# Sparse attention and a sentence-level mixture of experts on one core: k and q loaded by two head pairs at a time, in another order of the work

## The chip, the cores and the metric

The kernel runs on one core of one Trainium2 chip. The metric is the device time of one execution in microseconds. A profile of one execution stands beside it; its span runs from the first to the last instruction of the program, and all times inside it count from the start of that span.

## The reference

There are 4 batches, 8 heads, 768 positions and a head dimension of 64. Attention looks at near positions and at block summaries:

```python
k_sum = k.reshape(B, H, nb, block, D).max(axis=3)      # block = 32, so nb = 24
v_sum = v.reshape(B, H, nb, block, D).mean(axis=3)
mask_l = np.abs(pos[:, None] - pos[None, :]) < window   # window = 16
scores_s = scale * np.einsum('bhsd,bhnd->bhsn', q, k_sum) + np.log(block)
...
a = softmax of [masked scores_l, scores_s];  out = a @ [v, v_sum]
```

The heads side by side are x (768 x 512 for each batch). A gate takes the mean of x over positions, multiplies it by a 512 x 8 matrix and picks one expert for the whole batch; the output is the gate's probability times relu(x W1) W2 of that expert, with W1 512 x 1024 and W2 1024 x 512. So the weights of a batch's expert can only be fetched when its attention is complete.

## The kernel before, in words

All work is cut into 622 (634 after the change) small operations. The function `Plan` (lines 85 to 168) holds them; a list of numbers, `ORDER` (line 22), gives the order in which they are emitted. `solve` walks that list with a planned duration for each operation; it decides which buffer of a pool an operation takes, whether ACT or DVE does it where both may, and how many idle matmuls (line 880, they keep TensorE busy) go ahead of an operation that the plan finds waiting. It doesn't reorder. Each engine then runs its own operations in the order of the list, and waits at the head of its queue for what is missing.

The operations of a batch, with the lines that profiles show:

- Loads on POOL's queue: k and q rows (`load_rows`, L241), v (`load_v`, L252), and after the gate the expert's weights in five pieces (`G_load`, W1 in three pieces, L754, W2 in two, L757). The weights' pieces hold feature groups 0 to 1, 2 to 3 and 4 to 7 of W1. Loads are issued in the fixed order of `FIRST` and `LOADS` (lines 1096 and 1097): for each batch k and q, then v, then the weights of the batch before. Every load casts float32 to bfloat16.
- `T_pair` (L419): for one pair of heads, 16 transposes of k and 16 of q on PE. It waits for the loads of its own pair only. `K_own` and `Q_all` (L429 on ACT, L431 on DVE) copy the two results out of PSUM; `K_rest` (L461 to L481, DVE) takes the block maxima and fills in borders. Batch 0 uses `T` (L403), `K_max` and `S_mm` (L560 to L582) in their place.
- `S_win` (L602): the scores of one pair and one half of the positions, into the only score buffer of PSUM. `S_exp` (L621, ACT) is the exponential, `S_mask` (L368, DVE) the window.
- `V_sum` (L519, PE), `V_out`, `V_edge` (L501, L503) and `V_copy` (L542): the block means of v, put beside v.
- `O_mm` (L637, PE), `O_norm` (L651, L656, DVE), `X_mm` (L671, PE), `X_out` (L680, ACT, with the sum over positions): the attention's output, normalized and transposed.
- The gate: `G_add` (L698, DVE, batch 0 alone), `G_mm` (L707, PE), `G_pick` (L720 to L731 on DVE, then one small exponential, L736, on ACT). Their place on ACT and DVE is that of `G_pick` in the list. The plan counts no time on ACT for it. `factors` (L359 to L361) and `blocks` (L381 to L388) are constants that DVE builds once.
- The expert: `H_mm` (L786, 4 matmuls for one feature group and one half of the positions, 16 such groups), `H_out` (relu, L805 on ACT, L803 on DVE), `Y_mm` (L814, half of the features for 128 rows, called half-Y below), `Y_out` (L833, L828), `Y_store` (L871, SP). The last 128 rows of batch 3 go out in two halves (`Z_mm` L843, `Z_out` L862 and L863). `G_bc` (L772, SP) spreads the gate's value over 128 partitions.

The attention of batch b+1 is mixed with the expert of batch b. Six PSUM buffers of the pool "one" serve everything but scores; a PE operation that takes one waits until its last user has copied it out. k and q have two buffers each, by batch.

The part that the change touches reads, before:

```python
if kind == "kq":
    loads_kq(b, "k", ALLP, 0.8, KQ)
    loads_kq(b, "q", ALLP, 0.8, KQ)
```

Of the kernel before, what the change touches and what calls it, by code (L numbers as in the profile page):

```python
# [19 lines left out]


ORDER = [
    19, 14, 0, 2, 3, 1, 20, 22, 5, 29, 15, 4, 6, 23, 8, 21, 31, 30, 7, 24, 33, 17, 9, 10,
    38, 25, 32, 26, 34, 40, 12, 47, 18, 35, 16, 98, 56, 11, 36, 99, 58, 37, 57, 60, 39, 27,
    49, 78, 42, 59, 13, 41, 100, 50, 48, 74, 79, 66, 28, 67, 43, 61, 44, 75, 51, 45, 70,
    101, 68, 63, 62, 64, 80, 82, 65, 46, 52, 71, 69, 72, 53, 86, 102, 103, 83, 54, 84, 90,
    81, 104, 73, 87, 55, 91, 76, 94, 95, 108, 77, 88, 85, 96, 92, 89, 109, 97, 105, 126,
    110, 93, 171, 172, 111, 112, 106, 117, 107, 173, 113, 120, 127, 128, 118, 114, 119, 175,
    177, 115, 176, 135, 144, 129, 121, 136, 145, 122, 116, 178, 187, 137, 185, 138, 179,
    147, 146, 123, 151, 193, 186, 149, 152, 148, 195, 124, 194, 180, 181, 125, 183, 153,  # L30
    139, 188, 140, 189, 203, 248, 196, 156, 141, 157, 182, 250, 207, 190, 150, 184, 205,
    154, 191, 142, 252, 130, 204, 143, 208, 215, 158, 249, 206, 131, 197, 155, 216, 132,
    133, 166, 167, 199, 211, 192, 209, 251, 253, 134, 168, 200, 213, 212, 161, 210, 201,
    198, 174, 254, 169, 170, 162, 159, 238, 202, 218, 160, 163, 164, 165, 265, 239, 319,
    268, 214, 320, 321, 256, 266, 267, 323, 274, 255, 219, 325, 269, 259, 324, 327, 329,
    275, 217, 257, 220, 228, 258, 270, 233, 326, 277, 283, 260, 276, 229, 240, 261, 234,
    286, 271, 328, 292, 284, 235, 272, 285, 331, 273, 333, 339, 230, 262, 293, 337, 334,
    297, 296, 263, 347, 294, 396, 335, 336, 278, 330, 264, 338, 279, 348, 295, 223, 340,
    355, 351, 304, 280, 298, 224, 352, 341, 281, 305, 282, 299, 287, 356, 225, 345, 300,
    398, 342, 301, 288, 359, 363, 309, 289, 346, 364, 306, 290, 310, 302, 243, 332, 307,  # L40
    357, 360, 311, 353, 291, 244, 303, 308, 354, 314, 400, 245, 358, 315, 246, 397, 399,
    343, 413, 344, 404, 416, 316, 414, 402, 422, 415, 361, 317, 405, 322, 401, 362, 365,
    381, 349, 407, 221, 318, 236, 425, 417, 350, 247, 418, 376, 312, 382, 419, 226, 377,
    403, 313, 386, 423, 241, 424, 227, 467, 468, 406, 469, 471, 420, 426, 378, 427, 231,
    431, 440, 441, 421, 442, 434, 473, 475, 383, 445, 470, 408, 477, 366, 409, 444, 242,
    391, 222, 387, 371, 232, 388, 410, 392, 237, 432, 472, 367, 452, 411, 433, 443, 428,
    453, 393, 481, 372, 429, 482, 412, 435, 474, 493, 485, 368, 430, 436, 479, 476, 454,
    373, 495, 483, 446, 494, 478, 496, 505, 497, 484, 498, 374, 457, 506, 458, 486, 447,
    384, 437, 509, 448, 369, 438, 491, 513, 487, 511, 510, 501, 449, 492, 450, 439, 488,
    462, 459, 512, 489, 460, 451, 502, 480, 455, 463, 503, 490, 394, 461, 499, 464, 389,  # L50
    456, 379, 465, 500, 385, 504, 524, 466, 544, 519, 514, 545, 390, 507, 546, 395, 370,
    508, 548, 539, 529, 540, 380, 515, 534, 525, 535, 520, 547, 526, 375, 549, 530, 550,
    551, 527, 562, 516, 560, 536, 552, 558, 531, 553, 541, 554, 566, 559, 563, 572, 582,
    568, 583, 528, 567, 570, 584, 569, 521, 571, 556, 561, 522, 588, 564, 586, 585, 578,
    587, 555, 565, 573, 523, 557, 574, 542, 532, 517, 579, 576, 606, 589, 601, 580, 575,
    518, 537, 596, 590, 591, 597, 533, 581, 598, 577, 599, 538, 607, 592, 543, 600, 611,
    608, 609, 602, 593, 612, 613, 594, 619, 620, 610, 616, 595, 603, 604, 614, 617, 605,
    615, 621, 618,
]


# [20 lines left out]
class Plan:  # L82
# [16 lines left out]
    def add(self, engs, fn, kind, prio, deps=(), takes=(), count=0):  # L99
        if isinstance(engs, tuple):  # L100
            engs = [engs]
        op = Op(engs, fn, prio, deps, takes)
        op.kind, op.count = kind, count
        op.idx = len(self.ops)
        self.ops.append(op)
        for s in op.takes:
            s.users.append(op)
        return op
# [64 lines left out]
def kernel(  # L173
# [64 lines left out]
    def load_rows(b, which, src, h0, h1):  # L238
        if (which, b) not in nat:
            nat[which, b] = ld.tile([PR, H, RR * D], BF16, name=f"{which}_nat")  # L240
        nc.gpsimd.dma_start(  # L241
            nat[which, b][:, h0:h1, :],
            src[b, h0:h1].rearrange("h (p r) d -> p h (r d)", r=RR),
        )
# [77 lines left out]
    def edges(i):  # L322

        def f(op):
            e = nc.gpsimd
            e.memset(kaugs[i][:, :, 0:1, 0:R_OWN], 0.0)
            e.memset(kaugs[i][:, :, NJ - 1 : NJ, R_POST:R_SUM], 0.0)
            e.memset(kaugs[i][:, :, :, NR:128], 0.0)
        return f
# [570 lines left out]
    def transfer(fn, issue, dur, deps=()):  # L900

        deps = list(deps)
        if len(lanes) >= 8:
            deps.append(lanes[-8])
        if last[0] is not None:
            deps.append(last[0])
        i = add(("pool", issue), fn, "load", 0, deps)
        last[0] = i
        q_ = add(("q", dur), None, "ring", 0, [i])
        lanes.append(q_)  # L910
        return i, q_

    def loads_kq(b, which, prs, issue, per):
        deps = [R["T" + which, b - 2, p] for p in range(NP) if b >= 2]
        src = {"k": k, "q": q}[which]
        _, t = transfer(
            lambda op: load_rows(b, which, src, 2 * prs[0], 2 * prs[-1] + 2),
            issue, per * len(prs), deps,
        )
        for p in prs:  # L920
            R["L" + which, b, p] = t

    def loads_v(b, prs, issue, per):
        deps = [R["O", b - 2, p, u] for p in prs for u in range(2) if b >= 2]
        deps += [R["Vs", b - 2, p] for p in prs if b >= 2]
        _, t = transfer(
            lambda op: load_v(b, 2 * prs[0], 2 * prs[-1] + 2),
            issue, per * len(prs), deps,
        )
        for p in prs:  # L930
            R["Lv", b, p] = t

    KQ, VV = 1.1, 2.25
    ALLP = list(range(NP))
# [93 lines left out]
    def gate(b):  # L1028
        gs = Slot("one")
        a = add(("dve", 0.1), G_add(b), "gate", -1000,  # L1030
                [R["x", b, p, u] for p in ALLP for u in range(2)])
        m = add(("pe", 0.25), G_mm(b), "gate", -1000, [a], [gs])
        p = add(("dve", 0.6), G_pick(b), "gate", -1000, [m])
        gs.users.append(p)
        rec = add(("dve", 0.15), G_rec(b), "gate", -900, [p])
        R["grec", b] = rec
        w = Slot("w")
        R["w", b] = w
        deps = [p]
        for i, (c0, c1) in enumerate(zip(W1CUTS, W1CUTS[1:])):  # L1040
            iss, t = transfer(G_load(b, 0, c0, c1), 2.2 if i == 0 else 0.8,
                              1.05 + 0.4 * (c1 - c0), deps)
            if i == 0:
                iss.takes.append(w)
                w.users.append(iss)
            for c in range(c0, c1):
                R["w1", b, c] = t
        for c in range(2):
            _, t = transfer(G_load(b, 1, 4 * c, 4 * c + 4), 0.8, 2.6)
            R["w2", b, c] = t  # L1050
# [66 lines left out]
    def load_now(what):  # L1117
        kind, b = what[:-1], int(what[-1])
        if kind == "e":
            for i in (0, 1):  # L1120
                R["edge", i] = last[0] = add(("pool", 1.2), edges(i), "load", 0, [last[0]])
            return
        if kind == "kq":
            loads_kq(b, "k", ALLP, 0.8, KQ)
            loads_kq(b, "q", ALLP, 0.8, KQ)
        elif kind in ("k", "q"):
            loads_kq(b, kind, ALLP, 0.8, KQ)
        elif kind == "v":
            loads_v(b, [0, 1], 2.2, VV)
            loads_v(b, [2, 3], 2.2, VV)  # L1130
        else:
            gate(b)
# [5 lines left out]
    for what in LOADS:  # L1138
        load_now(what)
        if what[:-1] in after:  # L1140
            after[what[:-1]](int(what[-1]))
# [32 lines left out]
```

## Time and profile before

| what | value |
|---|---|
| median of 3 runs | 163.21 us (162.63 to 163.76) |
| the profiled execution's own time | 163.21 us |
| its span | 161.5 us |
| mean granted TensorE clock | 0.983 |
| k and q loads of batches 1 to 3 | 6 of 768 KB, median 14.5 us (k) and 17.6 us (q) from issue to landing |
| v of batch 0, second half, landed | 22.5 us |
| gate matmuls of batches 0 to 3 (L707) | 34.0, 61.2, 98.0, 127.2 us |
| first expert matmul, end of the last matmul | 41.2 us, 157.2 us |
| idle matmuls (L880) | 48, 14.5 us busy |

In the profile PE is TensorE's matmuls, PEld its weight loads, DVE VectorE, ACT ScalarE, POOL GpSimd and SP SyncE; a "q" behind a name is that engine's instruction queue. "128x512<-128x512 x18 | 12.4, 687" reads: output and input sizes, 18 instructions, 12.4 us busy in all, 687 ns each. An arrow in brackets names what ended a wait. The slices of the page are 40 equal parts of the span, and a digit is a share in tenths.

### The profile page before, as it was taken

What the parts mean: (1) busy time and instruction counts of PE and PEld (TensorE: products, weight loads), DVE (VectorE), ACT (ScalarE), POOL (GpSimd) and SP (SyncE); (2) the same over time, 40 slices, a digit from 0 to 9 for tenths busy, and PEclk for the clock granted to TensorE, in tenths of its full rate; (3) what the DMA queues carried; (4) which work ended last, traced back from release to release, by engine and by line L of the source; (5) the groups of instructions that cost most, each with busy time, mean ns of one, the idle gap of its engine ahead of it and who ended that gap; (6) DMA issues with size and microseconds to landing.
All of it is one profiled execution on the core that took longest, in us unless ns stands there. A gap on an engine that the chain in (4) does not pass through costs nothing.

```text
span 161.5 us, 4894 instructions
## 1 busy us (share of the span) xinstructions
PE 148.8 (92%) x2088; PEld 87.9 (54%) x2088; DVE 101.4 (63%) x288; ACT 90.3 (56%) x170; POOL 41.2 (26%) x58
## 2 busy tenths in 40 slices
PE   6798979989999997999999995999999999999990
PEld 2354657665556665555565753645667445565450
DVE  4387799679996844999786985686686231431010
ACT  3233447678778667796766764546668305352430
POOL 6997300009930001991000001700000080000000
PEclk9999999999999999999999999599999999999997
DMA  2999999998999999999999991999750059996135
GB/s 17 197 173 164 149 199 201 154 126 92 150 204 207 208 169 138 163 199 198 206 205 158 144 341 53 123 151 207 224 212 4 0 69 140 224 253 227 60 136 195
DMA packets 58581, 26.01 MB, mean 161 GB/s; under 512 B 38976, under 2 KB 55616, under 8 KB 58560
## 3 DMA queue, kind: packets, MB, share of 16 engines
q0 software_dynamic: 53856, 19.40, 132.2%
q1 hardware_dynamic: 4704, 6.31, 11.2%
q8 instruction: 16, 0.26, 0.7%
q14 instruction: 5, 0.04, 0.1%
HBM read 38.81 MB, written 6.29 MB: 279 GB/s over the span
## 4 chain that ended last, share of the span: by engine, by line
PE 70%; DMA 14%; POOL 4%; ACT 3%; issue 3%; DVE 2%; POOLq 0%; DVEq 0%; ACTq 0%
PE hps L786 24%; PE o_ps L814 21%; DMA vblk<-in_v_dram 9%; DMA w_sb<-in_moe_w_dram 5%; PE tps L419 5%; PE ops L637 4%; PE sc L602 4%; PE xps L671 4%; PE vsps L519 3%; PE idle_ps L880 3%; POOL vblk L252 1%; ACT aT L621 1%; PE o_ps L843 1%; POOL k_nat L241 1%; POOL q_nat L241 1%
## 5 line engine op out<-in xcount | busy, mean ns | idle before, releaser
L786 PE MATMUL hps<-xT,w_sb 128*128 128x384 bf16 x256 | 46.0, 327 | 0.2 <-DMA w_sb<-in_moe_w_dram 0.2
L814 PE MATMUL o_ps<-w_sb,hT 128*128 128x512 bf16 x184 | 43.9, 385 | 0.0
L621 ACT ACTIVATE aT<-sc 128x768 bf16<-128x768 f32 x32 | 25.9, 808 | 14.4 <-PE sc L582 8.8
L786 PEld LDWEIGHTS <-w_sb 128*128 128x128 bf16 x256 | 23.4, 98 | 15.8 <-DMA w_sb<-in_moe_w_dram 0.6
L754 POOL DMA_DIRECT2D w_sb<-in_moe_w_dram x12 | 9.0, 759 | 90.1 <-DVE kmt L461 37.3
L805 ACT ACTIVATE hT<-hps 128x384 bf16<-128x384 f32 x44 | 21.0, 491 | 15.3 <-PE hps L786 15.2
L814 PEld LDWEIGHTS <-hT 128*128 128x128 bf16 x184 | 17.2, 99 | 18.8 <-issue 1.1
L833 ACT ACTIVATE o_sb<-o_ps,gcol 128x512 f32<-128x512 f32 x18 | 12.4, 687 | 13.7 <-PE o_ps L814 13.6
L803 DVE TENSOR_SCALAR hT<-hps 128x384 bf16<-128x384 f32 x20 | 10.8, 554 | 14.3 <-PE hps L786 14.3
L656 DVE TENSOR_TENSOR xs<-ops,rv 128x384 bf16<-128x384 f32 x32 | 17.8, 558 | 1.1
L680 ACT ACTIVATE xT<-xps 128x768 bf16<-128x768 bf16 (+1 forms) x20 | 13.5, 681 | 5.0 <-PE xps L671 5.0
L252 POOL DMA_DIRECT2D vblk<-in_v_dram x10 | 15.8, 1596 | 0.8 <-issue 0.8
L880 PE MATMUL idle_ps<-zb 128*128 128x512 bf16 x48 | 14.5, 428 | 1.6 <-DVE zb L272 1.3
L368 DVE TENSOR_TENSOR aT<-aT,seen 96x1536 bf16<-96x1536 bf16 x12 | 11.3, 950 | 1.8 <-ACT aT L621 1.7
L429 ACT COPY qT<-tps 128x768 bf16<-128x768 bf16 x13 | 10.3, 793 | 0.9 <-PE tps L403 0.5
L602 PE MATMUL sc<-qT,kaug 64*128 64x64 bf16 x288 | 8.5, 193 | 2.3 <-ACT aT L621 2.3
L828 DVE TENSOR_SCALAR o_sb<-o_ps,gcol 128x512 f32<-128x512 f32 x5 | 3.7, 747 | 10.9 <-PE o_ps L814 10.9
L651 DVE RECIPROCAL rv<-ops 128x6 f32<-128x6 f32 x32 | 6.1, 190 | 6.6 <-PE ops L637 6.2
L637 PEld LDWEIGHTS <-aT 120*64 120x64 bf16 x384 | 7.6, 111 | 4.5 <-issue 3.3
L602 PEld LDWEIGHTS <-kaug 64*128 64x128 bf16 x288 | 5.8, 96 | 7.7 <-issue 6.4
L542 DVE COPY vblk<-vs_sb 24x1536 bf16<-24x1536 bf16 x16 | 9.7, 611 | 0.4
L637 PE MATMUL ops<-vblk,aT 120*64 120x65 bf16 x384 | 9.7, 197 | 0.3 <-DVE vblk L503 0.3
(93 smaller groups left out, 163.4 us busy)
## 6 DMA issues: line engine op xcount, KB each, us to landing
w_sb<-in_moe_w_dram POOLq DMA_DIRECT2D x12, 512.0 KB, 9.9
out_dram<-o_sb SPq DMA_DIRECT2D x23, 256.0 KB, 3.4
vblk<-in_v_dram POOLq DMA_DIRECT2D x6, 576.0 KB, 21.8
k_nat<-in_k_dram POOLq DMA_DIRECT2D x3, 768.0 KB, 14.5
q_nat<-in_q_dram POOLq DMA_DIRECT2D x3, 768.0 KB, 17.6
w_sb<-in_moe_w_dram POOLq DMA_DIRECT2D x8, 256.0 KB, 5.2
vblk<-in_v_dram POOLq DMA_DIRECT2D x2, 564.0 KB, 16.8
k_nat<-in_k_dram POOLq DMA_DIRECT2D x2, 384.0 KB, 5.6
```

The lines of the kernel that those rows point to most:

```text
L252: nc.gpsimd.dma_start(vb[p0:p1, n0:n1, 0:D], bass.AP(v.tensor, v.offset + ((b * H * NJ + n0) * QB - HALO + p0) * D, [[D, p1 - p0], [QB * D ...
L368: nc.vector.tensor_tensor(out=rows, in0=rows, in1=seen.unsqueeze(1).to_broadcast([R_SUM, 2 * NJ, QB]), op=ALU.mult,)
L602: nc.tensor.matmul(sc[:, hh, w * QB : (w + 1) * QB], lhsT=ka[rs, pr, j, :], rhs=qT[rs, j * QB : (j + 1) * QB], start=True, stop=True, tile ...
L621: nc.scalar.activation(aT, scs.pop((b, pr, u)), ACT.Exp, scale=SCALE)
L637: nc.tensor.matmul(ops[w * QB : (w + 1) * QB, t, hh, :], lhsT=weights(b, pr, hh, j), rhs=vb[0:NR, 2 * pr + hh, j, 0 : D + 1], start=True, ...
L656: nc.vector.tensor_tensor(out=xss[s][:, t0 : t0 + NW // 2], in0=ops[:, :, :, 0:D], in1=rv.unsqueeze(3).to_broadcast([128, NW // 2, 2, D]), ...
L680: nc.scalar.activation(xT[b][:, pr, us[0] * HB : (us[-1] + 1) * HB], xpss.pop((b, pr, us[0])), ACT.Copy, accum_out=red[b][:, pr, us[0] : u ...
L786: nc.tensor.matmul(hps[:, 0:HB], lhsT=w1_sb[:, dt, ft * 128 : (ft + 1) * 128], rhs=xT[b][:, dt, u * HB : (u + 1) * HB], start=(dt == 0), s ...
L805: nc.scalar.activation(dst, hps[:, 0:HB], ACT.Relu)
L814: nc.tensor.matmul(o_ps, lhsT=hTs[b][:, ft, st * 128 : (st + 1) * 128], rhs=wts[b][1][:, ft, :], start=(ft == 0), stop=(ft == NFT - 1),)
L833: nc.scalar.activation(o_sb, o_ps, ACT.Copy, scale=gcols[b][:, 0:1])
L880: nc.tensor.matmul(idle_ps[0], lhsT=zb[:, 0:128], rhs=zb, start=True, stop=True)
```

## The change

For batches 1 to 3 the loads of k and q go by two head pairs: k of pairs 0 and 1, q of pairs 0 and 1, k of pairs 2 and 3, q of pairs 2 and 3. There are four loads of 384 KB for each of these batches in place of two of 768 KB. Since the operations' numbers shift, and since the list was found again, `ORDER` is another list throughout, with 634 entries in place of 622; the operations on PE, ACT, DVE and SP are the same in number and kind but for one idle matmul fewer (47). Some go to ACT in place of DVE or the other way, as `solve` decides.

```diff
 ORDER = [
-    19, 14, 0, 2, 3, 1, 20, 22, 5, 29, 15, 4, 6, 23, 8, 21, 31, 30, 7, 24, 33, 17, 9, 10,
...
-    615, 621, 618,
+    19, 14, 0, 2, 1, 29, 3, 4, 5, 31, 6, 8, 30, 15, 21, 16, 32, 33, 7, 20, 22, 34, 10, 38,
...
+    606, 621, 616, 628, 607, 610, 611, 622, 629, 617, 612, 631, 630, 632, 633,
 ]
...
         if kind == "kq":
-            loads_kq(b, "k", ALLP, 0.8, KQ)
-            loads_kq(b, "q", ALLP, 0.8, KQ)
+            for prs in ([0, 1], [2, 3]):
+                loads_kq(b, "k", prs, 0.75, KQ)
+                loads_kq(b, "q", prs, 0.75, KQ)
```

The changed order on PE around the gates, written by operation (b.p is batch and pair; "half-Y" is one `Y_mm`):

```
batch 2 first:  ... O 1.2, H, O 1.3, T 2.0, X 1.1, half-Y, H, X 1.2, H, X 1.3, half-Y, half-Y, S 2.0,
                T 2.2, T 2.1, gate 1, S 2.0, T 2.3, 5 half-Y, S 2.1, V_sum 2, ...
batch 3 first:  ... O 2.3, T 3.0, half-Y, H, H, H, half-Y, S 3.0, T 3.1, X 2.1, X 2.3, half-Y, T 3.2, S 3.0,
                half-Y, half-Y, gate 2, S 3.1, half-Y, T 3.3, S 3.1, 4 half-Y, V_sum 3, S 3.2, ...
```

In the order before, the gates' surroundings are:

```
gate 1:  ... T 2.1, half-Y, gate 1, T 2.0, T 2.2, half-Y, S 2.1, ...
gate 2:  ... S 3.1, half-Y, half-Y, gate 2, S 3.2, T 3.3, V_sum 3, ...
```

On DVE the block maxima of pair 3 of batch 0 move behind `V_edge` of pairs 2 and 3, and `factors` from the start to between the sum and the pick of gate 0. The instructions on ACT, in the changed order, after the exponential of gate 2 are a k copy of pair 3 and an exponential of pair 1; the two ahead of it are a k copy of pair 2 and an exponential of pair 1.

## The prediction

> **What bounds the kernel now.** I read the page's busy table and slices first, then the chain that ended last, then the timeline around the chain's pauses, then the granted clock by window. The busy table and the slices:
>
> ```profile
> PE 148.8 (92%) x2088; PEld 87.9 (54%) x2088; DVE 101.4 (63%) x288; ACT 90.3 (56%) x170; POOL 41.2 (26%) x58
> ...
> PEclk9999999999999999999999999599999999999997
> ```
>
> TensorE is busy 92% of the span and no other engine is above 63%, so time is lost where PE stops or runs slowly. Its clock has one hole, slice 25 (about 101 to 105 us). The chain agrees: after 22.5 us, when the second half of v of batch 0 has landed, it is nearly all PE. From the first expert matmul (L786, 41.24 us) to the last (157.24) PE pauses at few places, nearly all at a gate. The worst is the gate of batch 2; the timeline there (start, duration, engine, line, wait in brackets):
>
> ```profile
> 95.85 0.35 PE L602 MATMUL sc<-qT,kaug 64*128 64x64 bf16 x12
> ...
> 97.96 0.34 PE L707 MATMUL lgps<-wg_sb,red 128*1 128x8 f32 x8
> ...
> 99.04 0.30 ACT L736 ACTIVATE ex<-lg,negm 1x8 f32<-1x8 f32 x1 [3.04 <-DVE negm L731]
> 99.24 0.18 ACT L736 ACTIVATION_READ_ACCUMULATOR ex<-lg,negm 1x1 f32 x1
> 99.34 0.78 ACT L621 ACTIVATE aT<-sc 128x768 bf16<-128x768 f32 x1
> ...
> 100.17 0.35 PE L602 MATMUL sc<-qT,kaug 64*128 64x64 bf16 x12 [1.86 <-ACT aT L621]
> ```
>
> The scores of 95.85 were complete at 96.2, but their exponential stands on ACT behind the gate's own small exponential, which waits for the gate matmul and five DVE steps. There is one score buffer, so PE's next scores wait till 100.17. What follows, by window (PEclk is the column after POOL):
>
> ```profile
> 98.30:100.17 1.87, 0.01 (x1) 0.03 (x1) 0.61 (x6) 1.13 (x4) 0.00 (x0) 1.00 0.04 15
> 100.17:101.70 1.53, 1.53 (x64) 1.41 (x67) 0.97 (x2) 1.21 (x2) 1.40 (x2) 0.87 0.00 0
> 101.70:104.40 2.70, 2.70 (x56) 1.59 (x45) 1.79 (x4) 1.61 (x3) 2.35 (x4) 0.50 1.14 146
> ```
>
> PE is full, at half clock. Price, from the chain: the v sum (48 matmuls) took 1.39 against 0.79 for batch 2, the scores 0.44 against 0.28, the 16 L814 matmuls 4.35 against 2 x 1.73: 0.60 + 0.16 + 0.89 = 1.65 us. The gate of batch 1 does the same to a k copy:
>
> ```profile
> 62.27 0.30 ACT L736 ACTIVATE ex<-lg,negm 1x8 f32<-1x8 f32 x1 [1.08 <-DVE negm L731]
> ...
> 63.40 0.53 PE L419 MATMUL tps<-identb,k_nat 96*64 96x96 bf16 x16 [1.05 <-ACT kaug L429]
> ```
>
> Two more PE pauses, 0.29 at 43.75 and 0.18 at 139.54, complete it: 1.05 + 1.86 + 1.65 + 0.29 + 0.18 = 5.03 us lost after 41.24.
>
> **What the Trainium skill says.** "TensorE: Matmul & The Clock Gate", Part 1, says ACT and DVE are strict FIFO; 99.04 above agrees. The same part gives an activity window of 3413 ns and a half-rate clock after an idle one, warning of gaps above some 3.4 us. Here a gap of 1.86 us was followed by the drop, so the measurement decides; the 1.05 us gap was followed by none. "DMA: Bandwidth & Descriptors", Queues, rings and completion order, says each DMA engine consumes descriptors in ring order; the trace agrees: k of batch 2, issued at 40.22, took 15.1 us to land (55.3), q, issued at 41.01, 18.3 us (59.3), in order, 4.0 us apart. Its Anatomy of one DMA (SWDGE) gives about 2.0 us fixed per DMA, mostly completion latency.
>
> **The change part by part.** (1) *Six more load issues.* k and q of batches 1 to 3 become 12 half loads. On POOL one issue takes 0.68 to 0.83 us (L241 rows), whatever its size, so each batch has 2 more, about 1.5 us, ahead of v. That is hidden: v of batch 2 is issued at 41.78 and lands at 64.2, and POOL waits 18 us or more before each gate's loads (19.1, 18.1, 27.0, 25.8 in the timeline). Without this cover v would be 1.5 us late. Fixed cost per extra DMA is between 0 (latency of queued transfers overlaps) and 2.0 us (that page's figure, an estimate); I take 0, since queued w loads of 512 KB land 2.55 us apart (46.05, 48.61, 51.16).
>
> (2) *What the halves free.* Transposes of pairs 0 and 1 need only the first two half loads. In batch 1 nothing was waiting for them (q lands at 29.5, transposes start at 30.5), in batch 3 neither (85.9 against 88.6). In batch 2 it matters: the new order puts a transpose ahead of the gate's work.
>
> (3) *The order at the gates.* In the changed order ACT has, at gate 2, the exponential of the last scores before the gate, and behind the gate's exponential a k copy that PE needs after two more half-Y groups (ready at 13.1 on the count below, wanted at 14.6) and an exponential that it needs after four and a v sum. Counted from the first transpose of batch 3: PE work up to the gate matmul is 10.15 us; the exponential of the scores ahead of it ends at about 9.3, the next scores' at 11.55, the gate's at 11.95, and PE's next scores come at 12.5. No wait. At gate 1 what stands behind it is a k copy (done about 2 us after the gate matmul), whose buffer PE takes after a transpose and four half-Y groups (over 4 us): no wait. So 1.05 + 1.86 + 1.65 go, and I take the 0.29 and 0.18 as gone too (V_edge and third w1 load have 0.4 and 0.8 us to spare): 5.03.
>
> (4) *Tile switches.* After 41.24 PE changes its tile position 66 times instead of 69; a switch costs 0.11 (first L786 group 0.76, others 0.65): 0.3 gained.
>
> (5) *The tail.* Before, the last output half is queued on SP behind two row stores (157.33, 157.77, then 158.30). Now those come before: issue at about 157.8 in the same frame, 0.5 gained.
>
> (6) *Gate 0 comes later.* The landing of v (22.51) doesn't move, nor does the v sum (done at 24.0). Then on DVE: vs copy 0.41, vblk copy 0.55, edge 0.45, and now also kmx of pair 3 (0.36 + 0.50 + 0.25), so scores of pair 3 start at 26.8 instead of 25.88. At the end DVE has the k copy of batch 1 (0.96), the last norm (0.75), K_rest (1.62), the gate's sum (0.15) and now the factors (0.94 in the timeline, 10.30 to 11.24) before it picks: about 35.1 instead of 34.38, +0.75. Every w load moves by this: first chunk 40.78 to 41.55, second 42.96 to 43.7. First L786: 41.24 to 41.65, +0.4. Its third group wants the second chunk at 43.4: +0.3. The first half loads of batch 2 follow: last w chunk 51.16 + 0.75, plus half of k and of q (2.05 each): 56.0. PE wants them after 14 H (0.65), 5 scores (0.28), 4 O (0.5), one X (0.34) and 7 switches: 13.6 us, at 41.65 + 0.3 + 13.6 = 55.55. Wait 0.5. Loss 1.2; bounds 0.3 (gate not late) to 3.2 (2 us fixed cost on q's half).
>
> (7) *Allowance.* Between 41 and 57 us DVE has 16.4 us of work against 20.5 of PE, with only some 0.4 us to spare at the first O and at two buffers. I charge 0.8, bounds 0 and 2.5.
>
> Sum: -5.03 - 0.3 - 0.5 + 1.2 + 0.8 = -3.8. Span 161.5 - 3.8 = 157.7; the profiled execution took 163.21, 1.7 around the span, and equals the median shown. Prediction 159.4 us.
>
> **Rivals.** *A, the waits move* (0.23): the order meets DVE lateness where I counted 0.4 us of slack; one PE pause of 1.9 us, and the half clock after it (1.65) as at 100 us. For: DVE is above 0.9 busy from 40 to 48 us before. Against: its work there isn't larger than before (16.4 against 16.5). 159.4 + 3.55 = 163.0. *B, slower* (0.14): the half loads share the DMA engines and land together, when q landed before, 59.3 + 0.75 = 60.05. The first transpose of batch 2 stands at PE's head from 55.55: wait 4.5 instead of 0.5, and half clock 1.65 after it: 159.4 + 4.0 + 1.65 = 165.05. It decides from a landing of about 59.8 on. Against: k and q landed in order and apart. *C, better* (0.08): neither (6) nor (7) costs anything: 157.4. *D, the split does nothing* and all is order: same time as mine, since of the split I only charge the 0.5; without it that wait would be B's.
>
> **How the numbers follow.** Likeliest (0.55) 159.4, its own range 158.0 to 161.2; C below, A at 161.6 to 164.5, B above. Leaving out B's upper part and the lowest of C gives 157.9 to 164.6. This kernel's measurement can tell 1% (1.6 us) from no change. Faster: likeliest + C = 0.63; within 1%: A, 0.22; slower 0.15.
>
> **What would show it.** Right: no PE wait on ACT at gates 1 and 2, no slice near 100 us with a low PEclk, gate 0 matmul or its pick 0.5 to 1 us later, first half of q of batch 2 landed near 56. Wrong: a PE pause above 1.5 us anywhere after 42 us with a clock drop behind it, or L419 waiting on q_nat for over 2 us.

## The result, and the profile after

The changed kernel takes 156.96 us (median of 4 runs, 156.71 to 157.40), against 162.92 us of the kernel before in the same runs (162.48 to 163.76): ratio 0.963, 95% interval 0.958 to 0.968. Ratios here and below leave out runs that are more than 1.5% above the fastest of their kernel, so they can differ from the quotient of the medians shown. The direction was as predicted, but the time is 2.4 us below the forecast and 0.9 below the range. The profiled execution took 156.81 us, its span is 154.8: 6.7 less than the span before. The forecast of the span was 157.7, so the miss is 2.9 us there; the forecast put 1.7 us around the span, and the profiled execution has 2.0.

The page after, busy times and granted clock:

```profile
PE 146.1 (94%) x2087; PEld 86.7 (56%) x2087; DVE 100.8 (65%) x291; ACT 89.5 (58%) x167; POOL 44.6 (29%) x64
...
PEclk9999999999999999999999999999999999999999
```

The hole of slice 25 is gone. The busy times by stretch say where 6.7 us went. The stretches are: start to first expert matmul (L786), from there to the end of the last matmul, and the rest. The first numbers are the length, then busy PE, PEld, DVE, ACT and POOL, then the clock. Before:

```profile
0.00:41.24 41.24, 36.18 (x644) 22.36 (x645) 30.79 (x105) 21.20 (x41) 19.87 (x36) 1.00 2.05 147
41.24:157.24 116.00, 112.59 (x1450) 65.53 (x1444) 70.66 (x185) 68.66 (x129) 21.34 (x23) 0.99 1.26 165
157.24:161.50 4.26, 0.00 (x1) 0.00 (x0) 0.00 (x0) 0.47 (x1) 0.00 (x0) 0.75 0.52 185
```

After:

```profile
0.00:40.82 40.82, 35.96 (x644) 22.09 (x644) 29.76 (x105) 22.13 (x41) 21.14 (x38) 1.00 2.01 150
40.82:151.44 110.62, 110.12 (x1450) 64.58 (x1444) 71.03 (x187) 66.91 (x125) 23.50 (x27) 1.00 1.35 175
151.44:154.80 3.36, 0.04 (x1) 0.00 (x0) 0.00 (x0) 0.47 (x1) 0.00 (x0) 1.00 0.43 151
```

The middle stretch is 5.38 us shorter, the start 0.42, the tail 0.90 (0.04 us of the last matmul lies behind the cut at 151.44, and spans are rounded to 0.1, so these sums are good to about 0.1 us). In the middle PE's idle time (length less busy) falls from 116.00 - 112.59 = 3.41 us to 0.50, by 2.91. Its busy time falls by 2.47, of which 1.65 is the half clock as the prediction priced it from the profile of before (no half clock is left after the change); 0.82 is left. Against the prediction's terms:

| part | predicted, us | measured, us |
|---|---|---|
| start to first expert matmul (step 6) | +0.4 | -0.42 |
| PE's pauses after it: -3.38 (step 3), +0.8 (step 6), +0.8 (step 7) | -1.78 | -2.91 |
| half clock (step 3) | -1.65 | -1.65 |
| rest of PE's busy time (step 4) | -0.3 | -0.82 |
| tail (step 5) | -0.5 | -0.90 |
| sum | -3.8 | -6.70 |

The timeline after, at gate 2, answers to the one at 95.85 to 100.17 us before:

```profile
95.94 0.34 PE L707 MATMUL lgps<-wg_sb,red 128*1 128x8 f32 x8
96.22 0.35 PE L602 MATMUL sc<-qT,kaug 64*128 64x64 bf16 x12
...
96.61 0.81 ACT L621 ACTIVATE aT<-sc 128x768 bf16<-128x768 f32 x1 [0.89 <-PE sc L602]
...
97.32 0.28 ACT L736 ACTIVATE ex<-lg,negm 1x8 f32<-1x8 f32 x1
...
98.04 0.80 ACT L429 COPY kaug<-tps 128x768 bf16<-128x768 bf16 x1 [0.35 <-PE tps L419]
...
98.27 0.35 PE L602 MATMUL sc<-qT,kaug 64*128 64x64 bf16 x12
```

ACT has the exponential of the scores ahead of the gate's small one, which finds its input ready (no bracket), and PE's next scores at 98.27 wait for nothing. Of PE's waits, by what ended them (total, times, longest), these two were there before and are not after:

```profile
PE sc L602 <- ACT aT L621: 2.3, 2, 1.9
...
PE tps L419 <- ACT kaug L429: 1.1, 1, 1.1
```

The longest one left after 41 us is new, at the first outputs of batch 1 (47.12 us), behind the window's mask on DVE:

```profile
PE ops L637 <- DVE aT L368: 0.4, 1, 0.4
```

### The profile page after: what moved, and what is told of

Read it like the earlier page. It is cut to its first block, busy times and chain, and to the rows that moved or that the text cites. A ratio compares the mean times of both kernels' runs of the same rounds, so it can differ in the third digit from the quotient of the medians.

```text
span 154.8 us, 4903 instructions
## 1 busy us (share of the span) xinstructions
PE 146.1 (94%) x2087; PEld 86.7 (56%) x2087; DVE 100.8 (65%) x291; ACT 89.5 (58%) x167; POOL 44.6 (29%) x64
## 3 DMA queue, kind: packets, MB, share of 16 engines
q1 hardware_dynamic: 4704, 6.31, 12.2%
## 4 chain that ended last, share of the span: by engine, by line
PE 76%; DMA 9%; DVE 6%; POOL 4%; ACT 1%; issue 1%; POOLq 0%
PE o_ps L814 26%; PE hps L786 25%; DMA vblk<-in_v_dram 9%; PE tps L419 5%; PE ops L637 4%; PE sc L602 4%; PE idle_ps L880 3%; PE xps L671 3%; PE vsps L519 3%; DVE vblk L542 2%; POOL vblk L252 2%; DVE aT L368 1%; PE o_ps L843 1%; POOL k_nat L241 1%; POOL q_nat L241 1%
## 5 line engine op out<-in xcount | busy, mean ns | idle before, releaser
L786 PE MATMUL hps<-xT,w_sb 128*128 128x384 bf16 x256 | 46.5, 327 | 0.0
L814 PE MATMUL o_ps<-w_sb,hT 128*128 128x512 bf16 x184 | 43.2, 379 | 0.0
L786 PEld LDWEIGHTS <-w_sb 128*128 128x128 bf16 x256 | 23.6, 98 | 15.6 <-DMA w_sb<-in_moe_w_dram 0.2
L805 ACT ACTIVATE hT<-hps 128x384 bf16<-128x384 f32 x43 | 20.4, 491 | 17.4 <-PE hps L786 17.2
L833 ACT ACTIVATE o_sb<-o_ps,gcol 128x512 f32<-128x512 f32 x16 | 10.9, 686 | 10.0 <-PE o_ps L814 8.0
L803 DVE TENSOR_SCALAR hT<-hps 128x384 bf16<-128x384 f32 x21 | 11.4, 553 | 7.4 <-PE hps L786 7.0
L828 DVE TENSOR_SCALAR o_sb<-o_ps,gcol 128x512 f32<-128x512 f32 x7 | 5.2, 750 | 13.1 <-PE o_ps L814 12.0
L429 ACT COPY qT<-tps 128x768 bf16<-128x768 bf16 x11 | 8.5, 796 | 1.5 <-PE tps L403 1.5
L651 DVE RECIPROCAL rv<-ops 128x6 f32<-128x6 f32 x32 | 6.1, 189 | 4.8 <-PE ops L637 4.7
L429 ACT COPY kaug<-tps 128x768 bf16<-128x768 bf16 x10 | 7.9, 793 | 1.0 <-PE tps L419 1.0
```

The lines of the kernel that those rows point to most:

```text
L429: nc.scalar.copy(out_, in_)
L786: nc.tensor.matmul(hps[:, 0:HB], lhsT=w1_sb[:, dt, ft * 128 : (ft + 1) * 128], rhs=xT[b][:, dt, u * HB : (u + 1) * HB], start=(dt == 0), s ...
L805: nc.scalar.activation(dst, hps[:, 0:HB], ACT.Relu)
L814: nc.tensor.matmul(o_ps, lhsT=hTs[b][:, ft, st * 128 : (st + 1) * 128], rhs=wts[b][1][:, ft, :], start=(ft == 0), stop=(ft == NFT - 1),)
```

## Experiments

The theory after the result: the gain is the order around the gates on ACT (with the half clock behind it) and the order of SP's last stores, and the prediction's two losses (steps 6 and 7) are covered. Its rivals: the split of the loads brings the gain by itself; something else in the new order does; or step 6 is a real loss that something unseen makes up for. Eight kernels were run, in two groups (E1 to E4, E5 to E8); the kernel before, run beside them, had medians of 164.21 us (39 runs) and 164.02 (23 runs), higher than above, so ratios and spans are compared, not medians of different groups.

**E1, the changed order with whole loads.** The list of operations stays; k and q of batches 1 to 3 are loaded whole in the place of their first halves.

```diff
-        _, t = transfer(
-            lambda op: load_rows(b, which, src, 2 * prs[0], 2 * prs[-1] + 2),
-            issue, per * len(prs), deps,
-        )
+        fn = lambda op: load_rows(b, which, src, 2 * prs[0], 2 * prs[-1] + 2)
+        if b:
+            fn = (lambda op: load_rows(b, which, src, 0, H)) if prs[0] == 0 else None
+        _, t = transfer(fn, issue, per * len(prs), deps)
```

> The changed order kept instruction for instruction, but k and q of batches 1 to 3 loaded whole again (k of all pairs, then q of all pairs). The gate theory (the gain is the order around the gates; the halves only feed the first transposes of batch 2 in time): one new wait, at the first transposes of batch 2, which stood at 54.9 us and now need all of q, landing at about 59.0. That is 4.0 us of wait, and 1.65 more if the clock halves behind it: 161.0 to 162.6 us. Gates 1 and 2 stay without a wait on ACT. The load theory (smaller loads by themselves bring the gain): waits come back in several places, the gates among them, and the time is that of the kernel before, 162.9.

Measured: 168.64 us (165.59 to 169.58, 4 runs); no ratio is on record. Both expectations are missed, on the slow side; the quickest run is still 8.2 us above the slowest of the changed kernel (157.40). The profiled execution took 168.99, with a span of 167.0, 12.2 more than with halves. PE's waits for q, then its timeline at both and the window behind the first one:

```profile
PE tps L419 <- DMA q_nat<-in_q_dram: 7.1, 2, 3.8
```

```profile
58.86 0.53 PE L419 MATMUL tps<-identb,q_nat 96*64 96x96 bf16 x16 [3.36 <-DMA q_nat<-in_q_dram]
...
60.72 1.49 PE L786 MATMUL hps<-xT,w_sb 128*128 128x384 bf16 x4
...
95.54 0.85 PE L419 MATMUL tps<-identb,q_nat 96*64 96x96 bf16 x16 [3.78 <-DMA q_nat<-in_q_dram]
```

```profile
60.40:63.90 3.50, 3.50 (x18) 1.96 (x17) 1.34 (x7) 1.76 (x5) 0.00 (x0) 0.52 3.94 142
```

PE's first transposes of q of batch 2 wait 3.36 us for the whole of q (landed 58.82), and 3.5 us at half clock follow: four L786 matmuls span 1.49 us instead of 0.82. That much was expected, and no wait on ACT came back at the gates. The second wait was not expected: PE waits 3.78 us more for the whole of q of batch 3, until 95.54, with a slow clock behind it. The lateness from the first wait is not its reason: loads and PE are both late by some 5.5 us there (k of batch 3 is issued at 74.07 instead of 68.44, its first transposes come at 91.23 instead of 85.74). The changed order takes the first transposes of batch 3 early too. With halves they run without a wait, 0.4 us after their half of q (85.67), while the rest of q lands at 90.18:

```profile
86.08 0.51 PE L419 MATMUL tps<-identb,q_nat 96*64 96x96 bf16 x16
```

The waits (7.1) and the clock lost (3.5 x 0.48 = 1.7 in this window, 7.0 x 0.41 = 2.9 from 95.5 to 102.5, where the mean clock is 0.59) make 11.7 of the 12.2. This profile is of one of the three longer executions. The quickest had a mean clock of 0.990 and a span of 163.6, 8.8 more than with halves; the same waits and about 1.6 us of lost clock (0.010 x 163.6) would make that, an estimate, since it was not profiled. So the changed order needs the halves. What B feared is what happens without them.

**E2, the order before with half loads, k and q in turn.**

```diff
...
+        if b:
+            def fn(op):
+                h = 0 if which == "k" else H // 2
+                load_rows(b, "k", k, h, h + H // 2)
+                load_rows(b, "q", q, h, h + H // 2)
```

> The order of before kept on PE, ACT, DVE and SP, with k and q of batches 1 to 3 in halves, in turn, as in the changed kernel. The gate theory: nothing waits for these loads in that order, so no change, 162.9 within 0.5. The load theory: most of the gain, 157 to 159.

Measured: ratio 1.001, interval 0.997 to 1.005 (163.92 us, 20 runs), span 161.8. Its timeline at gate 2:

```profile
98.61 0.35 PE L707 MATMUL lgps<-wg_sb,red 128*1 128x8 f32 x8
100.82 0.35 PE L602 MATMUL sc<-qT,kaug 64*128 64x64 bf16 x12 [1.86 <-ACT aT L621]
```

The wait is there unchanged. The split alone brings nothing and its extra issues cost nothing, both within the interval's 0.4% (some 0.65 us).

**E3, the order before, the gate's exponential later.** It is issued with the reciprocal of its sum (L762), behind the attention's work that it held up.

```diff
-            nc.scalar.activation(
-                out=ex8, in_=lg, func=ACT.Exp, bias=negm[0:1, 0:1], scale=1.0 / S,
-                accum_out=se,
-            )
...
             grec = small.tile([1, 1], FP32, name="grec")
+            nc.scalar.activation(
+                out=ex8, in_=lg, func=ACT.Exp, bias=negm[0:1, 0:1], scale=1.0 / S,
+                accum_out=se,
+            )
```

> The order of before, whole loads; only the gate's small exponential on ACT is emitted later, with the reciprocal that uses it, so that the score exponential and the k copy no longer stand behind it. The gate theory: the waits of 1.05 and 1.86 us at gates 1 and 2 go, and with them the half clock (1.65): 162.92 - 4.56 = 158.4. If the order around the gates is not the cause and the waits only move to the next thing that is late: 161 to 163.

Measured: ratio 0.981, interval 0.972 to 0.991 (159.95 us, 4 runs), span 157.7, 3.8 less. Its timeline at gate 2:

```profile
97.12 0.34 PE L707 MATMUL lgps<-wg_sb,red 128*1 128x8 f32 x8
...
97.79 0.81 ACT L621 ACTIVATE aT<-sc 128x768 bf16<-128x768 f32 x1 [0.69 <-PE sc L602]
...
99.27 0.35 PE L602 MATMUL sc<-qT,kaug 64*128 64x64 bf16 x12
...
100.26 0.30 ACT L759 ACTIVATE ex<-lg,negm 1x8 f32<-1x8 f32 x1
```

One small instruction moved on one queue takes away the waits at both gates and, in this profile, the half clock. The gain is 0.76 below the expected 4.56; PE has new waits of 0.26 (whole q of batch 2, at 60.17) and 0.64 (an output on DVE, at 135.67), which outweigh that. The gate theory stands.

**E4, the order before, the wait of gate 2 filled.** The wait stays; nine matmuls of 384 columns into the gate's own bank keep PE at work in it.

```diff
-            nc.vector.tensor_copy(lg, lgpss.pop(b)[0:1, 0:E])
+            lgps = lgpss.pop(b)
+            nc.vector.tensor_copy(lg, lgps[0:1, 0:E])
+            if b == 2:
+                for _ in range(9):
+                    nc.tensor.matmul(
+                        lgps[:, 128:512], lhsT=zb[:, 0:128], rhs=zb[:, 0:384],
+                        start=True, stop=True,
+                    )
```

> The order of before with the wait left in place at gate 2, but filled on PE with 9 matmuls of 384 columns into an unused part of the gate's own bank (9 x 0.163 = 1.5 us). If the wait is what halves the clock: clock 1.0 throughout, wait as before, 162.92 - 1.65 = 161.3. If the clock drop has another cause, or comes by chance: clock below 0.99 again and 162.9.

Measured: ratio 0.995, interval 0.991 to 0.999 (162.47 us, 20 runs), span 160.4. Timeline, and the window that follows:

```profile
98.84 1.62 PE L724 MATMUL lgps<-zb 128*128 128x384 bf16 x9 [0.24 <-DVE lg L721]
...
100.46 0.35 PE L602 MATMUL sc<-qT,kaug 64*128 64x64 bf16 x12
```

```profile
100.46:104.00 3.54, 3.38 (x111) 2.56 (x112) 2.67 (x5) 2.73 (x5) 3.42 (x5) 1.00 0.66 76
```

The scores come as late as before, and the clock stays at 1.00. From those scores to the end of the last matmul it is 156.11 - 100.46 = 55.65 us, against 157.24 - 100.17 = 57.07 before: 1.42 less, near the 1.65 priced. One profile could be luck, so the mean clocks of all executions count here: in 51 of 62 executions of the kernel before it is 0.990 or less (1.000 in the 11 others), in all 20 of E4 it is 0.993 or more. So the gap causes the drop, in most executions. A mean clock doesn't say where the clock was low: one execution of four has 0.989 in E3, and one in E7, whose profiles don't have this gap. Nor is 1.65 us shown as the price in each: in the first group the 8 executions of before with a clock of 1.000 are on average 2.1 us shorter than the 31 others, in the second group the 3 are no shorter than the 20. The ratio gains 0.5%, the medians of all runs 1.1% (164.21 to 162.47); 1.65 us would be 1.0%. E5 shows an execution without the drop.

**E5, the order before, row stores ahead of the last half outputs on SP.** Three entries of the list move up.

```diff
-    600, 611, 608, 609, 602, 593, 612, 613, 594, 619, 620, 610, 616, 595, 603, 604, 614,
+    600, 611, 608, 609, 602, 593, 612, 613, 594, 603, 604, 614, 619, 620, 610, 616, 595,
```

> The kernel before; on SP the two row stores of batch 3 stand ahead of both stores of the last half outputs, as in the changed kernel, all else as before. If the tail's gain comes from this queue, the end of the last matmul stays at 157.2 in a span of 161.5, and the time from there to the end falls from 4.26 to 3.4 to 3.8 us: 0.5 to 0.9 us less in all, ratio 0.995 to 0.997. If the tail's gain has another source (an earlier output copy on ACT), the tail stays at 4.2 us and the ratio is 1.000.

Measured: ratio 0.992, interval 0.988 to 0.996 (163.38 us, 20 runs), span 161.2; the interval reaches into the expected 0.995 to 0.997. The end of the timeline before, and of E5:

```profile
156.91 0.33 SPq L863 DMA_DIRECT2D out_dram<-o_half  x1
157.28 0.47 ACT L862 ACTIVATE o_half<-o_ps,gcol 128x256 f32<-128x256 f32 x1 [0.40 <-PE o_ps L843]
157.33 0.88 SPq L871 DMA_DIRECT2D out_dram<-o_sb  x2
158.30 0.40 SPq L863 DMA_DIRECT2D out_dram<-o_half  x1
```

```profile
157.26 1.21 SPq L863 DMA_DIRECT2D out_dram<-o_half  x2
157.63 0.47 ACT L862 ACTIVATE o_half<-o_ps,gcol 128x256 f32<-128x256 f32 x1 [0.40 <-PE o_ps L843]
```

Before, two row stores are issued (0.88 us) between the last half output and its store. In E5 the store is issued right behind the copy, and the tail from the last matmul takes 161.20 - 157.60 = 3.60 us instead of 4.26: 0.66 less. The kernels with this order of stores (the changed one, E1, E5 to E8) have tails of 3.3 to 3.6, those without (before, E2 to E4) 4.2 to 4.3. The same execution shows something else: the wait at gate 2 is in it, in full, but no half clock behind it.

```profile
102.31 0.35 PE L602 MATMUL sc<-qT,kaug 64*128 64x64 bf16 x12 [1.86 <-ACT aT L621]
...
103.39 0.85 PE L519 MATMUL vsps<-vblk,bind 96*32 96x128 bf16 x48
```

The v sum takes 0.85 us, where the same view of before has 1.46 (the prediction's 1.39 is the chain's count). So the drop does not follow this wait in each execution, and its 1.65 us is not paid in each.

**E6, the changed kernel, gate 0 relieved.** The block maxima of pair 3 and `factors` go where DVE waits for v. The numbers of idle matmuls are fixed to those of the changed kernel, so that the plan doesn't change them.

```diff
-    61, 51, 75, 101, 44, 45, 79, 102, 80, ... 69, 50, 82, ... 175, 17, 176, 115,
+    61, 51, 75, 101, 44, 45, 79, 50, 17, 102, 80, ... 69, 82, ... 175, 176, 115,
```

> The changed kernel; on DVE the block maxima of pair 3 of batch 0 and the three steps of the factors go into the stretch before v lands, in which DVE has time, so that neither stands between v and the pick of gate 0. The prediction's step 6 says that they put the pick off by 0.75 us and cost 1.2 us: then the pick comes 0.75 us sooner after v's landing (11.66 us after it in the changed kernel, 10.9 here) and the time is some 156.0. The reading of the changed kernel's trace (they are covered by DVE's wait for the gate matmul) says that the pick comes within 0.2 us of 11.66 after v, and that the time is the changed kernel's within 0.3 us (156.9).

Measured: 157.12 us (156.96 to 158.87, 4 runs), ratio 0.964, interval 0.949 to 0.979, the changed kernel's time. Span 155.2. The pick after, and in E6 with the first wait of DVE behind v:

```profile
33.73 0.15 DVE L720 COPY lg<-lgps 1x8 f32<-1x8 f32 x1 [0.27 <-PE lgps L707]
```

```profile
27.35 0.20 DVE L651 RECIPROCAL rv<-ops 128x6 f32<-128x6 f32 x1 [1.14 <-PE ops L637]
...
33.92 0.15 DVE L720 COPY lg<-lgps 1x8 f32<-1x8 f32 x1 [0.85 <-PE lgps L707]
```

v landed at 22.07 in the one and at 22.49 in the other, so the pick comes 11.66 and 11.43 us after it: 0.23 sooner, not 0.75. Most of the time that DVE saves turns into waiting: 1.14 instead of 0.15 us for the first attention output (L651) and 0.85 instead of 0.27 for the gate matmul. No run is below 156.96, where step 6 would give 156.0: its loss was not there to be removed.

**E7, the changed kernel with the later exponential of E3.** The edit is E3's, with the changed order:

```diff
-            gcols[b] = (lg, se)
+            gcols[b] = (lg, negm)
...
-            nc.vector.reciprocal(grec, gcols[b][1])
+            nc.vector.reciprocal(grec, se)
```

> The changed kernel; the gate's small exponential on ACT is issued later, with the reciprocal of its sum, so that nothing of a batch's attention stands behind it. If the changed order has removed all that the gate's exponential cost, nothing is left to gain: within 0.3 us of the changed kernel, 156.9. If gates in the changed kernel still hold back ACT, 0.5 to 1 us less. If the later exponential makes the gate's value late for the outputs (it waits on DVE for 0.99 us already at gate 1), 0.3 to 1 us more.

Measured: 158.66 us (158.35 to 159.18, 4 runs), ratio 0.969, interval 0.959 to 0.980; 1.5 us more than E6 in the same group by the medians. The two intervals overlap: three runs of E6 are below all of E7, the fourth (158.87) is not. DVE ahead of the pick of gate 2, after and in E7:

```profile
95.89 0.75 DVE L828 TENSOR_SCALAR o_sb<-o_ps,gcol 128x512 f32<-128x512 f32 x1 [0.99 <-DMA gcol<-grec]
```

```profile
98.03 0.75 DVE L829 TENSOR_SCALAR o_sb<-o_ps,gcol 128x512 f32<-128x512 f32 x1 [2.00 <-DMA gcol<-grec]
```

The value of gate 1 now lands later, the output copy on DVE waits 1.01 us longer for it, and the pick of gate 2 stands behind that copy. The weights of batch 2 are issued 100.64 - 97.08 = 3.56 us after the gate matmul instead of 98.50 - 95.94 = 2.56, and PE waits for a transpose's buffer (0.16 at 98.83) and for the third piece of the weights (0.32 at 110.82). This is the third case of the expectation, and by the medians larger than it said. The middle stretch is 112.55 us, 1.93 longer than in the changed kernel: 0.48 are these two waits, 0.55 is a longer wait for the window's mask at 48.19, which the later exponential doesn't explain, and the rest is in small pieces. So a loss is likely, with its path shown in the profile, and its size is explained only in part. What helps the order before by 3.8 us does not help the changed one: there the gates hold nothing up.

**E8, both small edits, E3 and E5, on the order before.** The diff is that of E5 and that of E3 together:

```diff
-    ... 594, 619, 620, 610, 616, 595, 603, 604, 614,
+    ... 594, 603, 604, 614, 619, 620, 610, 616, 595,
...
-            gcols[b] = (lg, se)
+            gcols[b] = (lg, negm)
```

> The kernel before with both of its small edits: the gate's exponential issued with the reciprocal, and the row stores ahead of the last half outputs. If the changed kernel's gain is the gates and the tail, the two add: 3.8 us (span, measured with the first alone) and 0.5 to 0.9: span 156.8 to 157.2, ratio 0.971 to 0.975. What is then left to the changed kernel's span of 154.8 (about 2 us) is what its order gains besides. If the two don't add, the span stays at 157.7.

Measured: 158.87 us (157.63 to 159.51, 4 runs), ratio 0.969, interval 0.956 to 0.982, span 157.8. Its stretches:

```profile
0.00:41.71 41.71, 35.91 (x644) 22.19 (x644) 30.33 (x102) 21.67 (x40) 19.47 (x35) 1.00 1.98 145
41.71:154.54 112.83, 111.03 (x1444) 64.63 (x1444) 71.91 (x187) 68.85 (x130) 21.74 (x24) 1.00 1.31 173
154.54:157.80 3.26, 0.00 (x1) 0.00 (x0) 0.00 (x0) 0.47 (x1) 0.00 (x0) 1.00 0.42 150
```

The two gains add (0.981 x 0.992 = 0.973; 0.969 measured): the two small edits bring 3.1% where E6, the changed kernel in all but gate 0, has 3.6% in the same group. The span is 0.6 above what was expected; it is the longest of the four (156.0 to 157.8), and in this execution v of batch 0 landed at 23.40 us, 0.9 later than before, so the start is 41.71. E6 is 1.75 us faster by the medians, though the intervals of the ratios overlap. In the profiles the rest is in the middle stretch, 112.83 against 110.24 us in E6: PE is idle for 1.80 against 0.15, and busy 0.94 longer, which is not explained. The idle time of E8 is waits for loads (0.71 for the whole of q of batch 2, 0.42 for weights) and 0.61 for `V_edge`. So part of what the new order and the halves bring beyond the two edits is that loads and borders are no longer late.

## Why the prediction was right, and where it was wrong

Of the miss of 2.9 us in the span, 1.2 is step 6, 0.4 an earlier landing of v, 0.3 step 7, 0.5 step 4 and 0.4 the tail.

**Step 1, right.** Six more issues cost nothing that shows: E2 has them and stands at 1.001 (0.997 to 1.005).

**Step 2 and rival B.** The halves of batch 2 landed at 53.09, 55.01, 56.92 and 58.92 us: in order, 1.9 to 2.0 us apart, where the whole loads of before landed 4.0 apart. So no fixed cost per load shows, and 0 was the right end of the bounds. The Trainium skill, "DMA: Bandwidth & Descriptors", Anatomy of one DMA (SWDGE), gives some 2.0 us fixed per DMA; in queued loads of this size none of it shows between landings. The ring order that the prediction quotes stands in the page's paragraph on the hardware queues, and these loads are issued by POOL; the landings here are the evidence. PE's transposes of k and q came without a wait, those of q 0.27 us after their half:

```profile
55.28 0.51 PE L419 MATMUL tps<-identb,q_nat 96*64 96x96 bf16 x16
```

Step 2's "in batch 3 neither" was wrong: it set the landing against the 88.6 us of the order before, but the changed order begins batch 3 at 85.74, and E1 shows a wait of 3.78 us there without the halves. B's premise, halves that land together, is refuted, and E1 shows that its mechanism is real: 3.36 us of wait at the same transposes, 3.5 us at half clock behind it, and a second wait.

**Step 3, right.** The waits of 1.05 and 1.86 us are gone, and so is the hole in the clock. E3 shows that the order on ACT was their cause, E2 that the loads were not, E4 that the gap causes the drop. The 1.65 us is what the profiled execution paid; the one of E5 paid nothing.

**Step 4, not settled.** 0.3 us was predicted for tile switches; 0.82 us of PE's busy time is left unexplained. E6 and E7, with the same order on PE, differ by 110.71 - 110.09 = 0.62 us in the same figure, so it cannot be assigned.

**Step 5, right, but its size too small.** The tail gave 0.90 us in place of 0.5, 0.66 in E5. The last store is issued 152.02 - 151.44 = 0.58 us after the last matmul instead of 158.30 - 157.24 = 1.06, 0.48 sooner, as predicted. What was left out is its landing: 1.70 us after the issue instead of 2.17 (153.72 and 160.47), with no two row stores just ahead of it.

**Step 6, wrong: the step that failed.** "At the end DVE has the k copy of batch 1, ... and now also the factors before it picks: about 35.1 instead of 34.38." That added the new work to DVE's queue from v to the pick, as if the waits in that queue were not there to absorb it. The pick came at 33.73. DVE's waits before, then DVE after:

```profile
29.05 0.20 DVE L651 RECIPROCAL rv<-ops 128x6 f32<-128x6 f32 x1 [0.76 <-PE ops L637]
...
30.28 0.20 DVE L651 RECIPROCAL rv<-ops 128x6 f32<-128x6 f32 x1 [0.44 <-PE ops L637]
...
34.38 0.15 DVE L720 COPY lg<-lgps 1x8 f32<-1x8 f32 x1 [0.71 <-PE lgps L707]
```

```profile
26.16 0.25 DVE L465 TENSOR_REDUCE kmx_line<-kmt 128x24 bf16<-128x96 bf16 x1
...
27.15 0.20 DVE L651 RECIPROCAL rv<-ops 128x6 f32<-128x6 f32 x1 [0.15 <-PE ops L637]
...
29.00 0.20 DVE L651 RECIPROCAL rv<-ops 128x6 f32<-128x6 f32 x1 [0.37 <-PE ops L637]
...
33.26 0.19 DVE L361 TENSOR_SCALAR seen<-d_k 96x64 bf16<-96x64 f32 x1
```

From the v sum to the pick DVE waited 0.76 + 0.44 + 0.71 = 1.91 us for PE before, and 0.15 + 0.37 + 0.27 = 0.79 after: the block maxima and the factors went into that time. Of the pair-3 scores only the last two matmuls (L582) need the block maxima; they waited 0.15 us, at 26.47. The factors took 0.66 us (32.79 to 33.45; the prediction took 0.94) and lay in a time when DVE would have waited for the gate matmul anyway. So what released the pick was the gate matmul on PE, not the end of DVE's own work. E6 confirms it: taking both pieces away brings 0.23 us there, and nothing in the whole. So 1.2 us of predicted loss were not there. The pick even came 0.65 us sooner than before, 0.44 of which is the earlier landing of v in that execution (22.07 against 22.51; the profiles here show 22.07 to 23.40), which is luck of that execution and not the change. The rest of step 6 hung on the late pick: neither the second piece of the weights nor the half of q was waited for.

**Step 7, too large.** 0.8 us was set aside for DVE's lateness between 41 and 57 us. PE pauses there for 0.15 us (41.79) and 0.36 us (47.12). In all, PE idles for 0.50 us in the middle stretch.

**Rivals.** A (waits move) did not happen: no wait above 0.4 us after 41 us. C (neither 6 nor 7 costs anything) was given 157.4 and 8 in 100. Its time is what happened, 0.4 us better still, by the tail, step 4 and the earlier v, though step 7 did cost some 0.5. D (the split does nothing) is right for the order before (E2) and wrong for the order after (E1), in two batches and not in one.

## What to carry to other kernels

On an engine that runs its queue in order, a tiny instruction with a late input can be the dearest one: price what stands behind it on its queue and who waits for that (here 0.30 us of work cost 1.05 + 1.86 us, and a half clock in most executions). Before charging work added to an engine's queue, find the next wait of that engine at the same place: work that fits in the wait is free, and only what is above it counts. A reordering and a split of loads may each be useless or harmful alone and right together, so test them apart in both directions. Test too whether a few small edits bring most of what a new order brings: two moves on single queues, in the old order, gave 3.1% where the whole change gave 3.6% (E8 and E6, whose intervals overlap).

## What was not expected of the hardware

A PE gap of 1.86 us was followed by half clock in the profiles of before (1.65 us lost) and E2, and by none in that of E5, with a gap of the same length at the same place. The mean clock is 0.990 or less in 51 of 62 executions of before, and in none of 20 where matmuls fill the gap (E4). The Trainium skill, "TensorE: Matmul & The Clock Gate", Part 1, says that the activity window (3413 ns) runs free and that the number of slow matmuls at a kernel's start varies with its phase; a gap that meets the window at different phases would agree with this, but no run here shows the window. That a gap of about half the window suffices goes against the bound quoted from that page in the prediction, and the measurement decides.
